# A weight transfer cut in two, and the products that fill the wait for it: gated attention and MLP decode step on one core

## The chip, the cores and the metric

One of the eight cores of a Trainium2 chip runs the kernel. The metric is the device time of one execution in microseconds (us). The kernel before takes 131.65 us (median of 3 runs, 131.53 to 131.69).

## The reference

One token (x of 576 numbers) goes through two branches, mixed by a gate: attention with 32 query heads on 16 cached key and value heads, of which the last 4096 positions are read, and an MLP with 4608 hidden units.

```python
q = x @ wq                                       # 576 -> 32 heads of 128
scores = q k^T * 128**-0.5                       # 4096 keys, two query heads per cache head
a = (softmax(scores) v).reshape(4096) @ wo       # wo: 4096 x 576
h = gelu(x @ w1 + b1)                            # 4608
b = h @ w2 + b2                                  # w2: 4608 x 576
g = sigmoid(sum(x * gate_w))
out = g * a + (1 - g) * b
```

Weights and caches are used once, in bf16. 53.6 MB come from memory; there is little arithmetic per byte.

## The kernel before: what the argument touches

All large loads go through one queue in this order: w1, wq, four tiles of K, two of V, half of w2, the third of V, the last rows of wo, the fourth of V, then the main part of wo (31 rows of 576 for each partition), then the other half of w2 in three pieces. The output y gathers in PSUM from many products. One product takes a column of 128 activations, one for each partition, and for each partition a row of 576 weights, and adds up over the partitions; it is done as two matmuls of 272 and 304 columns.

```python
    def y_add(vec, row, start=False, stop=False):
        for s in range(2):
            last = nc.tensor.matmul(
                y_out[s], lhsT=vec,
                rhs=row[:, DH:D] if s else row[:, 0:DH], ...   # cut
            )
        return last
    # ... cut: the attention, and the loads listed above
    RO = RW                                              # 31
    wo_t = big.tile([P, RO, D], BF16, name="wo_t", tag="D")
    nc.sync.dma_start(                                   # one transfer, 4464 KB
        out=wo_t[:].rearrange("p r n -> p (r n)"),
        in_=wo_src[:, 0 : 4 * RW, :].rearrange("h (a r) n -> h a (r n)", a=4),
    )
    for j0, j1 in ((0, 10), (10, 16), (16, 18)):         # w2, second half
        nc.sync.dma_start(out=w2_t[:, NJ + j0 : NJ + j1, :], in_=w2_src[:, 1, j0:j1, :])
    # ... cut: six w2 products, and the small ones that make ov from the attention's output
    late = [(gt, f, w2_t[:, f, :]) for f in range(6, NJ)]        # 12 products, loaded long ago
    wo_at = [(ov, r, wo_t[:, r, :]) for r in range(RO)]          # 31 products
    w2_at = [(gt, f, w2_t[:, f, :]) for f in range(NJ, NF)]      # 18 products
    late += [(ov_tail, j, wo_tail[:, j, :]) for j in range(4)]
    late.append(None)                                    # the unused product
    late += wo_at + w2_at
    # TensorE does `late` in this order; None is a 128 x 512 fp32 matmul
    # into a PSUM tile (spare_ps) that nobody reads
```

A product needs its row to be in SBUF, so TensorE waits, in this order, for wo and for the three w2 pieces. The list's order is forced.

## Time and profile before

| | before |
|---|---|
| span of the profiled run | 130.3 us |
| moved by DMA | 53.75 MB, 413 GB/s on average |
| TensorE busy with matmuls | 81.5 us (63%) |
| VectorE busy | 52.0 us (40%) |
| mean granted TensorE clock (share of full speed) | 0.856 |

No engine is busy throughout, but the 16 DMA engines nearly are. The lines that carry this are in the prediction and not shown again. One caution for reading them: the trace's clock records begin at 45.08 us, and up to there the views show full clock whatever it was.

### The profile page before, as it was taken

Reading aid. Unit: us, or ns where it says so; the run is one execution under the profiler, and the core shown is the slowest. Engines: PE = TensorE matmul, PEld = TensorE weight load, DVE = VectorE, ACT = ScalarE, POOL = GpSimd, SP = SyncE. Lnnn points to the kernel's source line nnn. Section 1 sums busy time; section 2 is a strip of 40 time slices with the busy share of each in tenths; the row PEclk is TensorE's granted clock in tenths of the full one; section 3 lists DMA queues with packets and bytes.
Section 4 is the critical chain, followed back from the end, with each engine's and each line's share of the span. In section 5 each row is a group of like instructions: output and inputs, shape, how many; then the busy total and the mean of one; then the engine's idle time right before and its main releaser. Section 6 shows DMA issues by size and latency. Waiting matters only on the chain.

```text
span 130.3 us, 2402 instructions
## 1 busy us (share of the span) xinstructions
PE 81.5 (63%) x1150; PEld 47.8 (37%) x1080; DVE 52.0 (40%) x48; ACT 8.3 (6%) x18; POOL 9.1 (7%) x24
## 2 busy tenths in 40 slices
PE   0019999375003998949909985985300830899994
PEld 0019949375000121211202121685300830865672
DVE  0234000400069969999999995604000020010001
ACT  2100000003000000030003003021000000000001
POOL 7049600000000000000000000000000000000000
PEclk9999999999999999999995899975555555555999
DMA  7999999899899999899999999899999989898980
GB/s 232 410 433 446 475 424 475 353 473 448 362 468 463 392 433 473 382 433 473 402 412 483 402 412 473 363 451 479 397 412 468 433 377 492 362 509 356 393 361 16
DMA packets 2364, 53.75 MB, mean 413 GB/s; under 512 B 270, under 2 KB 274, under 8 KB 564
## 3 DMA queue, kind: packets, MB, share of 16 engines
q1 hardware_dynamic: 2346, 53.61, 96.4%
q8 instruction: 8, 0.13, 0.4%
q10 hardware_dynamic: 10, 0.01, 0.0%
HBM read 53.62 MB, written 0.00 MB: 412 GB/s over the span
## 4 chain that ended last, share of the span: by engine, by line
DMA 52%; DVE 24%; PE 13%; issue 6%; SPq 2%; ACT 0%
DMA k_t<-in_A_k_cache_dram 27%; DMA w_t<-in_B_w_dram 25%; DVE kt L529 19%; PE s_ps L551 7%; PE o_ps L638 5%; DVE m L567 3%; DVE pt L600 2%; SPq L686 1%; PE y_ps L394 1%; DVE mr L570 1%; SPq L681 0%; PE mt_ps L576 0%; SPq L234 0%; ACT out_row L742 0%; SPq L230 0%
## 5 line engine op out<-in xcount | busy, mean ns | idle before, releaser
L551 PE MATMUL s_ps<-kt,qz_flat 128*128 128x512 bf16 x128 | 32.4, 410 | 17.4 <-DVE kt L529 10.6
L529 DVE STREAM_TRANSPOSE kt<-k_t 128x4096 f32<-128x4096 f32 x8 | 35.3, 4431 | 11.9 <-DMA k_t<-in_A_k_cache_dram 10.7
L638 PE MATMUL o_ps<-pt,v_t 128*128 128x8 bf16 x512 | 14.2, 167 | 16.9 <-DMA v_t<-in_A_v_cache_dram 14.9
L551 PEld LDWEIGHTS <-qz_flat 128*128 128x128 bf16 x64 | 6.8, 106 | 40.4 <-issue 38.9
L638 PEld LDWEIGHTS <-v_t 128*128 128x128 bf16 x512 | 14.1, 102 | 17.7 <-DMA v_t<-in_A_v_cache_dram 15.1
L422 PEld LDWEIGHTS <-w_t 128*128 128x128 bf16 x162 | 10.2, 165 | 0.5 <-issue 0.4
L422 PE MATMUL h_ps<-x,w_t 128*128 128x2 bf16 x162 | 10.4, 202 | 0.0
L394 PE MATMUL y_ps<-w_t,gt 128*1 128x272 bf16 (+1 forms) x72 | 8.0, 363 | 0.1
L588 ACT ACTIVATE p_t<-s_ps,negm 128x1024 bf16<-128x1024 f32 x4 | 4.5, 1114 | 50.9 <-DVE negm L584 50.9
L668 DVE RECIPROCAL rg<-mt_ps 128x32 f32<-128x32 f32 x1 | 0.4, 358 | 15.7 <-PE mt_ps L663 15.7
L343 PE MATMUL xs_ps<-ident,rows 1*128 1x1 bf16 x9 | 0.6, 189 | 9.4 <-POOL ident masks.py:199 9.4
L600 DVE STREAM_TRANSPOSE pt<-p_t 128x1024 bf16<-128x1024 bf16 x4 | 4.9, 1223 | 2.7 <-ACT p_t L588 2.7
L460 PE MATMUL q_ps<-x,wq_t 128*128 128x2 bf16 x144 | 4.0, 166 | 3.0 <-DMA wq_t<-in_A_wq_dram 3.0
L394 PEld LDWEIGHTS <-gt 128*1 128x1 bf16 x72 | 4.5, 97 | 2.2 <-issue 0.7
L567 DVE TENSOR_REDUCE m<-s_ps 128x1 f32<-128x1024 f32 x4 | 4.8, 1194 | 1.1 <-PE s_ps L551 1.1
L460 PEld LDWEIGHTS <-wq_t 128*128 128x128 bf16 x144 | 3.9, 104 | 3.0 <-DMA wq_t<-in_A_wq_dram 3.0
L743 DVE CAST out_row<-y_ps 1x272 bf16<-1x272 f32 x1 | 0.4, 429 | 11.4 <-PE y_ps L394 11.4
L431 DVE COPY hacc<-h_ps 128x36 f32<-128x36 f32 x1 | 0.2, 195 | 11.4 <-PE h_ps L422 11.4
L394 PE MATMUL y_ps<-wo_t,ov 128*1 128x272 bf16 (+1 forms) x62 | 4.2, 286 | 0.1
L343 PEld LDWEIGHTS <-rows 1*128 1x128 bf16 x9 | 0.7, 150 | 9.3 <-DVE rows L337 6.6
L394 PEld LDWEIGHTS <-ov 128*1 128x1 bf16 x62 | 3.4, 84 | 1.3 <-issue 0.8
L689 DVE TENSOR_TENSOR om<-o_ps,rgh 128x128 bf16<-128x128 f32 x1 | 0.3, 292 | 8.8 <-PE o_ps L638 8.8
(72 smaller groups left out, 38.1 us busy)
## 6 DMA issues: line engine op xcount, KB each, us to landing
k_t<-in_A_k_cache_dram SPq DMA_DIRECT2D x4, 4096.0 KB, 32.2
v_t<-in_A_v_cache_dram SPq DMA_DIRECT2D x4, 4096.0 KB, 24.9
wq_t<-in_A_wq_dram SPq DMA_DIRECT2D x1, 4608.0 KB
wo_t<-in_A_wo_dram SPq DMA_DIRECT2D x1, 4464.0 KB
w_t<-in_B_w_dram SPq DMA_DIRECT2D x1, 2880.0 KB, 14.3
w_t<-in_B_w_dram SPq DMA_DIRECT2D x1, 2592.0 KB, 23.3
w_t<-in_B_w_dram SPq DMA_DIRECT2D x1, 2304.0 KB, 8.1
w_t<-in_B_w_dram SPq DMA_DIRECT2D x1, 1440.0 KB
```

Source lines behind the costliest of these rows:

```text
L343: nc.tensor.matmul(xs_ps[:, i, :], lhsT=xdup[:, i : 2 * D : NI], rhs=ident[0:1, 0:1], start=(i == 0), stop=(i == NI - 1), skip_group_check ...
L394: last = nc.tensor.matmul(y_out[s], lhsT=vec, rhs=row[:, DH:D] if s else row[:, 0:DH], start=start, stop=stop, skip_group_check=True,)
L422: nc.tensor.matmul(h_ps[:, j:NF:NJ], lhsT=w1_t[:, i, j:FH:NJ], rhs=x2[:, i, :], start=False, stop=(i == NI - 1 and j == NJ - 1), skip_grou ...
L460: nc.tensor.matmul(q_ps[:, j : Hq : Hq // 2], lhsT=wq_t[:, i, j * Dh : (j + 1) * Dh], rhs=x2[:, i, :], start=(i == 0 and j == 0), stop=(i ...
L529: lambda: nc.vector.transpose(out=kt[g, f][:].bitcast(FP32), in_=keys.rearrange("p c d -> p (c d)").bitcast(FP32),),
L551: last = nc.tensor.matmul(s_ps[g][:, u * 512 : (u + 1) * 512].rearrange("p (c k) -> p c k", k=32), lhsT=qz(g, j, 2 * f + half), rhs=kv[:, ...
L567: queue("dve", lambda: nc.vector.reduce_max(out=m1[:], in_=s_ps[g][:], axis=AX.X))
L570: lambda: nc.vector.tensor_scalar(out=mr[:], in0=hi16[:], scalar1=m1[:, 0:1], scalar2=None, op0=ALU.mult),
L588: nc.scalar.activation(out=p_t[:].rearrange("p c k -> p (c k)"), in_=s_ps[g][:], func=ACT.Exp, bias=negm[:, 0:1], scale=SCALE, accum_out=s ...
L600: lambda: nc.vector.transpose(out=pt[:, g, :, :].rearrange("p c q -> p (c q)"), in_=p_t[:].rearrange("p c k -> p (c k)"),),
L638: last = nc.tensor.matmul(o_ps[:, 8 * g : 8 * g + 8, 0], lhsT=v_t[g][:, c, :], rhs=pt[:, g, c % 32, 8 * (c // 32) : 8 * (c // 32) + 8], st ...
L686: nc.sync.dma_start(out=w2_t[:, NJ + j0 : NJ + j1, :], in_=w2_src[:, 1, j0:j1, :])
```

## The change

Its intent: the unused product kept TensorE at work while wo was in flight. If wo comes in two transfers, its first rows are there sooner, and eight real products can do that duty. Eight more (rows 8 to 15) are held back for the later gaps, while w2 is in flight.

```diff
-    nc.sync.dma_start(
-        out=wo_t[:].rearrange("p r n -> p (r n)"),
-        in_=wo_src[:, 0 : 4 * RW, :].rearrange("h (a r) n -> h a (r n)", a=4),
-    )
+    for r0, r1 in ((0, 16), (16, RO)):
+        nc.sync.dma_start(
+            out=wo_t[:, r0:r1, :].rearrange("p r n -> p (r n)"),
+            in_=wo_src[:, 0 : 4 * RW, :].rearrange("h (a r) n -> h a (r n)", a=4)[
+                :, :, r0 * D : r1 * D
+            ],
+        )
...
-    spare_ps = ps_s.tile([P, 1024], FP32, name="spare_ps", tag="s")
-    late.append(None)
-    late += wo_at + w2_at
+    late += wo_at[0:8] + wo_at[16:RO] + wo_at[8:13] + w2_at[0:10] + wo_at[13:16] + w2_at[10:]
...   (the matmul into spare_ps goes from the loop)
```

## The prediction

> **What bounds the kernel now.** I read the 40 slices first, then the chain of waits, then the timeline of the last 20 us, then the semaphore and packet records. The slices (PE is busy share of TensorE in tenths, DMA the mean busy share of the 16 DMA engines):
>
> ```profile
> PE   0019999375003998949909985985300830899994
> PEclk9999999999999999999995899975555555555999
> DMA  7999999899899999899999999899999989898980
> ```
>
> DMA stands at 8 or 9 tenths from the second slice to the last but one; TensorE has long holes. 53.75 MB in 130.3 us is 413 GB/s. So this is a stream from memory, and a change on TensorE counts only if it shortens what follows the last byte. The chain of waits (start us, us, what) says what follows it:
>
> ```profile
> 93.11 1.53 SPq L686
> 94.64 0.05 issue
> 94.69 32.72 DMA w_t<-in_B_w_dram
> 127.41 0.04 issue
> 127.45 1.21 PE y_ps L394 x16
> 128.66 0.02 issue
> 128.69 0.40 ACT out_row L742
> ```
>
> The end is made of the landing of a piece of w2 at 127.41, then 16 matmuls (1.21 us), a copy out of PSUM (0.40 us) and the store. The products with wo are not in the chain's last part at all. The timeline of the end shows how TensorE gets there (start, busy us, instructions, idle before in brackets):
>
> ```profile
> 116.85 3.20 PE L394 MATMUL y_ps<-w_t,gt 128*1 128x272 bf16 x24
> ...
> 119.98 0.75 PE L394 MATMUL y_ps<-zeros,ov_tail 48*1 48x272 bf16 x8
> 120.66 0.30 PEld L730 LDWEIGHTS spare_ps<-p_t,ones 128*128 128x128 f32 x2 [0.27 <-issue]
> 120.66 1.13 PE L730 MATMUL spare_ps<-p_t,ones 128*128 128x512 f32 x2
> 121.72 3.76 PEld L394 LDWEIGHTS <-ov 128*1 128x1 bf16 x60 [0.76 <-issue]
> 121.90 3.78 PE L394 MATMUL y_ps<-wo_t,ov 128*1 128x272 bf16 x59
> ...
> 127.45 0.86 PEld L394 LDWEIGHTS <-gt 128*1 128x1 bf16 x15 [0.43 <-issue]
> ```
>
> The unused product (two fp32 passes) fills 120.66 to 121.79, while wo is still in flight. The first wo product starts at 121.90; the trace's semaphore records (not a line of the page) put wo's landing at 121.86. They put the three last w2 pieces at 125.32 (rows 0 to 10), 127.41 (10 to 16) and 128.08 (16 to 18). What matters is the bracket of the last line: before the last 16 matmuls TensorE already waits 0.43 us for a transfer. It has slack now.
>
> **What the Trainium skill says.** "DMA: Bandwidth & Descriptors", section "Why a DMA increments its semaphore by 16 and not by 1": each of the 16 engines ends its share with its own write to the semaphore, so a transfer is there when its slowest engine is through. The trace agrees: 270 packets under 512 B, almost all 4-byte writes, 16 to a large transfer. The same page, "Rules for kernel authors", asks for 1 MiB or more per DMA. Both new pieces, 2304 and 2160 KB, stay above that. The same page[...] fits a fixed cost of about 2.0 us per DMA; in this queue the trace does not show it between transfers: the packet records have the next transfer's first packet on an engine starting within 3 ns of the 4-byte write before it. "TensorE: Matmul & The Clock Gate", Part 1, says the clock is halved by default and is decided in free-running windows of 3413 ns. The trace agrees: one half-clock stretch is 3.413 us, another 34.133 us, ten windows. In such windows (us, then PE busy; the granted clock is the fraction ahead of the DMA share):
>
> ```profile
> 65.55:68.97 3.42, 0.66 (x4) 0.11 (x2) 3.42 (x3) 0.56 (x1) 0.00 (x0) 1.00 0.98 422
> 68.97:72.38 3.41, 3.41 (x10) 0.59 (x5) 3.41 (x1) 0.64 (x2) 0.00 (x0) 0.50 0.91 394
> ...
> 75.79:79.21 3.42, 2.06 (x11) 0.68 (x6) 3.42 (x1) 0.00 (x0) 0.00 (x0) 1.00 1.05 450
> 79.21:82.62 3.41, 3.06 (x15) 0.67 (x7) 1.60 (x3) 1.21 (x2) 0.00 (x0) 1.00 1.07 461
> ...
> 116.75:120.17 3.42, 3.42 (x31) 1.82 (x29) 0.19 (x1) 0.15 (x1) 0.00 (x0) 0.50 1.05 451
> 120.17:123.58 3.41, 3.29 (x38) 2.10 (x36) 0.00 (x0) 0.00 (x0) 0.00 (x0) 1.00 0.88 365
> ```
>
> A window with 0.66 us of matmul is followed by half clock; one with 2.06 us is not; the busy window 116.75 to 120.17 brings full clock at 120.17, before the unused product starts at 120.66.
>
> **The change, part by part.** The columns stay split 272 and 304, so no product changes shape.
>
> (1) The wo transfer of 4464 KB (128 packets of 35712 B) becomes two, 128 packets of 18432 B and 128 of 17280 B, in the same place of the queue. The bytes are the same. In the packet records of this trace a packet of 36864 B took 1364 ns and one of 18432 B 686 ns, so halving a packet costs 2 x 686 - 1364 = 8 ns. Each engine has 8 such packets and one more 4-byte write (9 ns): 8 x 8 + 9 = 73 ns, an estimate and rather high, as neighbouring records overlap by 3 to 4 ns. I take 0.06 us. All of it is on the path: everything behind wo in the queue lands that much later.
>
> (2) The first piece lands early. The V transfer ahead of it landed at 111.3; 8 packets of 686 ns are 5.5 us, so about 116.9. TensorE wants it at 120.7: no wait.
>
> (3) The unused product goes (1.13 us) and 8 products, 16 matmuls, take its place. In the wo block matmuls start every (125.49 - 121.90) / 62 = 58 ns, so 16 take 0.93 us and run from 120.7 to 121.65. TensorE then waits some 0.3 us for the second piece, at 121.86 + 0.06 = 121.92.
>
> (4) After it stand 15 + 5 = 20 products, 40 matmuls, 2.3 us, to 124.25, where before 62 matmuls ran to 125.5. TensorE then waits for rows 0 to 10 of w2 until 125.32 + 0.06 = 125.38: a new idle gap of 1.1 us.
>
> (5) 20 matmuls with w2 (1.2 us) to 126.55, then the 3 held products (6 matmuls, 0.35 us) to 126.9, then a wait of 0.5 to 0.6 us for rows 10 to 16, at 127.41 + 0.06 = 127.47.
>
> (6) The last 16 matmuls, the copy and the store are as before. The last 4 matmuls need the last piece at 128.08 + 0.06 = 128.14; TensorE reaches them after 12 matmuls, 127.5 + 12 x 0.058 = 128.2, so that piece is not the limit, though only by 0.06 us.
>
> (7) One more transfer on the SP queue shifts the round of semaphores by one. The built program shows that the last w2 piece now waits, before it is issued, for the third V transfer, which landed at 101.3. Its data are wanted at 128: nothing lost, as the queue is full till then.
>
> Sum: +0.06 us on the DMA path, about 1 us of TensorE time freed, all of it into waits. 131.65 + 0.06 = 131.7.
>
> **Rivals.** *TensorE gains count.* About 1.2 us less work stands behind wo's second piece; were TensorE the bound, the time would be near 130.5. For it: the wo block runs without a hole from 121.9 on. Against it: the 0.43 us wait at 127.45, which ends on a landing. I give it almost nothing.
>
> *The clock falls back.* TensorE now idles in three gaps (0.3, 1.1 and 0.55 us). If the window 123.58 to 126.99 were judged idle, the last 16 matmuls would run at half clock: 24 of them took 3.20 us so at 116.85, 133 ns each, or 16 x 133 = 2.1 us in place of 1.21, so 132.6. Against it: I expect 0.67 + 1.55 = 2.2 us busy in that window, above the 2.06 us that kept full clock; the windows run free of the kernel, but no gap here comes near the 2.75 us idle of the window that lost it. The eight held products are there for this.
>
> *The second transfer pays a fixed cost.* If the skill's 2 us stood open at the seam, 133.7. Against it: the packets of 3 ns distance named above. Smaller harm, 0.2 to 0.5 us, could come from an uneven pace of the 16 engines, as a half-size packet changes their phase.
>
> **Range and chances.** Three runs of before lie within 0.16 us, and my sum moves by 0.06. Below there is little room: the bytes bind. Above, the clock rival and a few tenths at the seam. I predict 131.7 us, 131.3 to 132.3 in eight cases of ten. Two per cent is 2.6 us, more than any rival makes: faster 0.01, within 0.97, slower 0.02.
>
> **What would show it.** Right: the last chain again ends with a DMA of w_t landing near 127.5 and 16 matmuls of about 1.2 us; first wo product at 120.7 with no wait; holes near 121.8, 124.3 and 127.0; granted clock 1.0 from about 120.2 to the end. Wrong: a last block of about 2 us (clock), a landing of w_t later than 127.8 (seam), or a last block that begins with no wait before it (TensorE the bound).

## The result, and the profile after

| | before | after |
|---|---|---|
| median of 6 runs each, us | 131.67 (131.53 to 131.69) | 131.73 (131.55 to 131.80) |
| ratio after / before | | 1.0004 (95%: 0.9991 to 1.0017): the same |
| DMA packets | 2364 | 2508 |
| span of the profiled run, us | 130.3 | 130.4 |

Ratios here are the mean time of one kernel's fast runs over that of the other's in the same rounds, so not quite the ratio of the medians quoted.

The chain of waits of the kernel after ends as that of before did; compare the three numbers of the landing, the block and the copy.

```profile
94.54 32.94 DMA w_t<-in_B_w_dram
127.48 0.04 issue
127.52 1.21 PE y_ps L394 x16
128.73 0.02 issue
128.75 0.40 ACT out_row L733
```

The landing is at 127.48 instead of 127.41, the block after it takes 1.21 us in both. The timeline of TensorE in the kernel after (start, busy us, instructions, idle before in brackets) shows where the rest went:

```profile
119.98 0.85 PE L394 MATMUL y_ps<-zeros,ov_tail 48*1 48x272 bf16 x8
...
120.77 3.96 PE L394 MATMUL y_ps<-wo_t,ov 128*1 128x272 bf16 x56
121.98 2.28 PEld L394 LDWEIGHTS <-ov 128*1 128x1 bf16 x38 [0.32 <-issue]
...
125.44 1.33 PE L394 MATMUL y_ps<-w_t,gt 128*1 128x272 bf16 x19 [0.71 <-DMA w_t<-in_B_w_dram]
125.44 1.12 PEld L394 LDWEIGHTS <-gt 128*1 128x1 bf16 x19 [1.05 <-issue]
...
127.52 0.86 PEld L394 LDWEIGHTS <-gt 128*1 128x1 bf16 x15 [0.58 <-issue]
```

The first wo product starts at 120.77 instead of 121.90 and follows the work ahead of it without a wait. Then come three holes, before 121.98, 125.44 and 127.52: the products done early bought waits of 0.3, 1.05 and 0.58 us. Read the weight loads (PEld) for the holes: a matmul's end is modelled, so a hole between matmuls looks shorter than the one between weight loads. In windows of 3.41 us laid on the trace's own clock events, the granted clock is full from 120.37 to the end:

```profile
116.96:120.37 3.41, 3.41 (x28) 2.12 (x26) 0.19 (x1) 0.16 (x1) 0.00 (x0) 0.50 0.98 421
120.37:123.78 3.41, 3.40 (x53) 2.60 (x50) 0.00 (x0) 0.00 (x0) 0.00 (x0) 1.00 1.01 419
123.78:127.19 3.41, 2.70 (x40) 1.87 (x36) 0.00 (x0) 0.00 (x0) 0.00 (x0) 1.00 0.85 347
```

### The profile page after: what moved, and what is told of

It reads as the page before. It is cut to its first block, busy times and chain, and to the rows that moved or that the text cites. A ratio compares the mean times of both kernels' runs of the same rounds, so it can differ in the third digit from the quotient of the medians.

```text
span 130.4 us, 2399 instructions
## 1 busy us (share of the span) xinstructions
PE 80.9 (62%) x1148; PEld 47.9 (37%) x1078; DVE 52.0 (40%) x48; ACT 8.3 (6%) x18; POOL 9.1 (7%) x24
## 2 busy tenths in 40 slices
DMA packets 2508, 53.75 MB, mean 412 GB/s; under 512 B 286, under 2 KB 290, under 8 KB 580
## 4 chain that ended last, share of the span: by engine, by line
DMA 52%; DVE 24%; PE 13%; issue 7%; SPq 2%; ACT 0%
DMA k_t<-in_A_k_cache_dram 27%; DMA w_t<-in_B_w_dram 25%; DVE kt L529 19%; PE s_ps L551 7%; PE o_ps L638 5%; DVE m L567 3%; DVE pt L600 2%; PE y_ps L394 1%; SPq L682 1%; DVE mr L570 1%; SPq L689 0%; PE mt_ps L576 0%; SPq L234 0%; ACT out_row L733 0%; SPq L230 0%
## 5 line engine op out<-in xcount | busy, mean ns | idle before, releaser
L394 PE MATMUL y_ps<-w_t,gt 128*1 128x272 bf16 (+1 forms) x72 | 7.5, 362 | 0.9 <-DMA w_t<-in_B_w_dram 0.9
```

The source lines that it names most:

```text
L394: last = nc.tensor.matmul(y_out[s], lhsT=vec, rhs=row[:, DH:D] if s else row[:, 0:DH], start=start, stop=stop, skip_group_check=True,)
```

## The experiments

The theory: the memory stream sets the end; the change puts about 0.06 us on the stream and moves TensorE's work about within its slack. The rivals: TensorE's work counts wherever it stands; the clock depends on the filled gaps; a cut costs much, and the new order hides that.

### Each half of the change alone

**split_only**: the two transfers, with the unused product and the old order.

```diff
 (the kernel before)
-    nc.sync.dma_start(out=wo_t[:]..., in_=...)
+    for r0, r1 in ((0, 16), (16, RO)): nc.sync.dma_start(...)      # as in the change
```

> The kernel before with only the wo transfer cut in two (16 and 15 rows); the unused product and the old order of products stay. Theory (the memory stream sets the end, a seam costs about 0.06 us of it): 131.67 + 0.06 = 131.7 us, the last w2 rows 10 to 16 land near 127.5, a wait of about 0.4 us stays ahead of the last 16 matmuls. Rival (a cut costs some tenths by upsetting the pace of the 16 engines, and the new order gives that back): 132.0 to 132.3 us.

Measured: 131.58 us (131.51 to 131.98, 6 runs) against 131.54 of before on the same chip; ratio 1.0003 (0.9990 to 1.0017). In its profile the landing ahead of the last 16 matmuls was at 127.25 and the block took 1.21 us: no hidden loss of the 0.3 to 0.6 us that the rival needs, and so nothing for the new order to give back. That this landing came before the 127.41 of the kernel before says that single profiles differ by more than the 0.06 us in question. One cut can't be read from one trace; wo_in_ten below measures it.

**order_only**, and the same kernel again as **order_only_b**: the new order without the unused product, wo in one transfer.

```diff
 (the kernel after)
-    for r0, r1 in ((0, 16), (16, RO)): nc.sync.dma_start(...)
+    nc.sync.dma_start(out=wo_t[:]..., in_=...)                     # one transfer, as before
```

> The changed kernel with wo in one transfer again: no unused product, the new order. TensorE idles from about 120.8 until wo lands at 121.9, then runs all it has. Theory: all of it is slack, 131.67 us within 0.1, granted clock 1.0 to the end. Rival (the unused product was needed to keep the clock up over that 1.1 us gap): half clock for a window from about 123.6 on, the wo block at some 133 ns a matmul instead of 58, about 4 us more work, and as it then runs past the landing, 133 us or more. Rival (TensorE's work counts): 130.5 to 131.2 us.

Measured: 131.70 us median, but in two groups: 131.42, 131.45, 131.68 and 131.72, and then 132.85 and 132.98. Neither answer fits: the theory gives the first group, and nothing said gave the second. Hence the repeat:

> The same kernel as order_only once more, for more executions and another profile: two of its six executions took 132.85 and 132.98 us, the other four 131.42 to 131.72, and no profile fell on a slow one. New theory (where the clock's 3.413 us windows fall against the empty stretch before wo decides it): again two groups, 131.4 to 131.8 and 132.7 to 133.1, at least one execution of the second; a profile of the second would show half clock for one window after 121.9. Rival (a disturbance of the chip in two executions): all six within 131.4 to 131.8.

Measured: 131.53, 131.56, 131.69, 131.71 and again 132.73 and 132.85. Of 12 executions 4 are slow by some 1.2 us, all of them within 0.25 us of each other; of 29 executions of the kernel before none took over 132.06. (All 12 lie within 1.5% of the fastest: 1.0032 and 1.0026 with intervals that hold 1.) This time the profile fell on a slow one. Its TensorE timeline, then its windows:

```profile
118.89 0.68 PE L394 MATMUL y_ps<-zeros,ov_tail 48*1 48x272 bf16 x8
121.81 4.89 PE L394 MATMUL y_ps<-wo_t,ov 128*1 128x272 bf16 x54 [2.23 <-DMA wo_t<-in_A_wo_dram]
```

```profile
114.39:117.81 3.42, 3.42 (x44) 2.04 (x40) 0.60 (x3) 0.15 (x1) 0.00 (x0) 0.50 0.95 402
117.81:121.22 3.41, 1.76 (x26) 1.09 (x22) 0.00 (x0) 0.00 (x0) 0.00 (x0) 1.00 0.93 401
121.22:124.63 3.41, 2.83 (x25) 2.17 (x26) 0.00 (x0) 0.00 (x0) 0.00 (x0) 0.50 0.99 408
124.63:128.04 3.41, 3.41 (x59) 2.73 (x55) 0.00 (x0) 0.00 (x0) 0.00 (x0) 1.00 0.64 257
```

The fractions 0.50 and 1.00 are the granted clock. Here the clock rose early, at 117.81, so TensorE was through with its work at 119.6 and sat idle for 2.23 us. That window, with 1.76 us of matmul, is followed by one at half clock, in which wo landed. The chain of waits of this run no longer ends on a landing:

```profile
92.40 29.36 DMA wo_t<-in_A_wo_dram
121.76 0.04 issue
121.81 7.88 PE y_ps L394 x84
```

From wo's landing on, TensorE works 7.88 us without a stop and is now the bound. In the profile of order_only, a fast execution, the clock rose 1.2 us later against the work, at 119.04, the idle stretch was 1.52 us, and the clock stayed at full. So the one slow profile shows what made that execution slow: half clock while the first wo products ran. That the idle stretch brought it is read from the order of the two windows, and that the other three executions have the same cause is inferred from their equal times. The unused product was not idle decoration: it filled most of this stretch. In the changed kernel, which differs from order_only in the cut alone, the first wo products fill it: of its executions and those of split_only and no_hold, which have the same cut, 0 of 18 are of the slow kind. The old order without the unused product was not run; the orders differ only behind wo's landing, while the stretch lies ahead of it.

### The stretch made deeper, and filled again

**gap_deep**: in order_only, six products on w2 rows that have long been loaded move from before wo's landing to after it.

```diff
 (order_only)
-    late = [(gt, f, w2_t[:, f, :]) for f in range(6, NJ)]
+    late = [(gt, f, w2_t[:, f, :]) for f in range(6, 12)]
+    held = [(gt, f, w2_t[:, f, :]) for f in range(12, NJ)]
...
-    late += wo_at[0:8] + wo_at[16:RO] + wo_at[8:13] + w2_at[0:10] + ...
+    late += wo_at[0:8] + wo_at[16:RO] + wo_at[8:13] + held + w2_at[0:10] + ...
```

> order_only with six more w2 products (12 matmuls) moved from before wo's landing to after the first 28 wo products: TensorE's empty stretch before 121.9 grows from 1.5 to about 2.5 us, the sum of its work does not change. New theory (a window with too little matmul work in it keeps or takes half clock): most or all executions at 133 to 134 us, and the profile shows granted clock 0.5 in a window after 121.9. Rival (the clock plays no part; only work behind the landing counts): 74 + 20 matmuls x 58 ns from 121.9 is 127.35, before the landing at 127.41, so 131.6 us.

Measured: 134.77 us (134.66 to 135.26, 4 runs), ratio 1.0248 (1.0224 to 1.0271), all executions slow, and by more than I had expected. Its windows:

```profile
116.61:120.02 3.41, 3.11 (x26) 1.46 (x23) 0.19 (x1) 0.15 (x1) 0.00 (x0) 0.50 1.04 449
120.02:123.43 3.41, 1.45 (x13) 1.21 (x14) 0.00 (x0) 0.00 (x0) 0.00 (x0) 0.50 0.87 362
123.43:126.85 3.42, 3.42 (x32) 2.55 (x29) 0.00 (x0) 0.00 (x0) 0.00 (x0) 0.50 0.90 371
126.85:130.26 3.41, 3.41 (x58) 2.46 (x54) 0.00 (x0) 0.00 (x0) 0.00 (x0) 1.00 0.08 30
```

The clock did not fall; it never rose, until a full window of work had passed after the landing. TensorE ran at half clock from 121.98 to 126.85, and its block after wo's landing lasted 9.65 us. The work and the stream are the same, and 3 us are lost.

**gap_filled**: gap_deep with two unused products in the stretch.

```diff
 (gap_deep)
-    late += wo_at[0:8] + ...
+    late += [None, None] + wo_at[0:8] + ...      # each None: the 128 x 512 fp32 matmul
```

> gap_deep (134.77 us) with two unused 128 x 512 fp32 products put into its empty stretch, nothing else changed: more work on TensorE, the same transfers, the same order. Theory (the stretch cost time only through the clock): full clock from about 120 on, and 131.6 to 132.0 us, some 3 us less than gap_deep although TensorE does 2.3 us more. Rival (what cost time in gap_deep was the six products moved behind wo's landing): 134.7 us or more.

Measured: 131.93, 132.45, 133.50 and 134.64 us; the last, the profiled one, counts as slow (over 1.5% above the fastest), the ratio of the other three is 1.0078 (1.0038 to 1.0119). So the filling helped, by 1.3 to 2.8 us in three executions of four against gap_deep's median, while it added work; that speaks against the rival. But my number held only for one of four. In the profiled execution the clock rose at 123.73 only, after a window with 3.41 us of fp32 matmul, and the filler itself, at half clock, held TensorE from 119.62 to 123.4, past wo's landing. A filler bought for the clock can cost what it was meant to save; products that must be done anyway add no work. I take this run as support for the clock's part, not as a clean proof.

### Are the held products needed?

**no_hold**: the changed kernel with its wo products in plain order.

```diff
-    late += wo_at[0:8] + wo_at[16:RO] + wo_at[8:13] + w2_at[0:10] + wo_at[13:16] + w2_at[10:]
+    late += wo_at + w2_at
```

> The changed kernel with the plain order (wo rows 0 to 31, then w2 rows): the eight products are not held, all 62 wo matmuls are done by about 124.4 and TensorE is empty until w2 lands at 125.4, and again from 126.6 to 127.5. Window from 123.8 to 127.2: about 0.6 + 1.2 = 1.8 us of work. Theory (holding buys no time where the clock stays; 1.68 and 2.06 us of work a window kept full clock in the kernel before): 131.7 us. Rival (the held products are needed for the clock): some executions with the last 16 matmuls at half clock, 2.1 us instead of 1.2, 132.6 us.

Measured: 131.74 us (131.57 to 131.99, 6 runs), ratio 1.0007 (0.9993 to 1.0022), no execution near 132.6. In the profile TensorE idles longer before both w2 landings and keeps full clock from 119.02 to the end. In these six executions holding eight products back bought nothing; it is the cut that makes the difference against order_only, as it gives TensorE 16 rows to work on during wo's second half. That some alignment of the windows, seen in none of the six, would need the held products is not excluded.

### What is on the path

**behind_last**: eight wo products moved behind the last w2 product.

```diff
-    late += wo_at[0:8] + wo_at[16:RO] + wo_at[8:13] + w2_at[0:10] + wo_at[13:16] + w2_at[10:]
+    late += wo_at[0:8] + wo_at[16:RO] + w2_at + wo_at[8:16]
```

> The changed kernel with the eight held wo products moved behind the last w2 product: the same transfers and the same work, 16 matmuls more behind the last landing. Theory (only what stands behind the last landing is on the path, at 58 ns a matmul): +0.93 us, 132.6 to 132.7 us. Rival (TensorE's total work sets the end wherever it stands): 131.7 us.

Measured: 132.75 us (132.71 to 132.88, 4 runs), ratio 1.0084 (1.0068 to 1.0101), or some 1.1 us more than before, about 1.0 more than the changed kernel. The chain shows it: the landing stays, the block grows from 1.21 to 2.25 us.

```profile
94.59 32.82 DMA w_t<-in_B_w_dram
127.42 0.04 issue
127.46 2.25 PE y_ps L394 x30
```

(30 instead of 32: some matmul records are missing from a trace.) The same eight products cost nothing ahead of the landing and a full microsecond behind it.

**less_wo**: 8 rows of wo less are loaded, with the same number of products (a wrong result, on purpose).

```diff
-    for r0, r1 in ((0, 16), (16, RO)):
+    for r0, r1 in ((0, 16), (16, RO - 8)):
...
-    wo_at = [(ov, r, wo_t[:, r, :]) for r in range(RO)]
+    wo_at = [(ov, r, wo_t[:, min(r, RO - 9), :]) for r in range(RO)]
```

> Wrong result on purpose: the second wo transfer brings 7 rows instead of 15, and the products of the missing rows use the last row there is, so TensorE's work is the same and 8 x 576 x 2 x 128 = 1.18 MB less is moved. Theory (the stream sets the end): [...]1.18 MB take 2.7 us, so about 129.0 us; if TensorE then comes on the path (its products between 121 and 127 need 62 + 36 matmuls x 58 ns = 5.7 us from 120.8, so 126.5 plus the gaps) a little more, up to 129.6. Rival (TensorE's chain of products sets the end): within 0.3 us of 131.7.

Measured: 129.50 us (129.10 to 130.31, 4 runs), ratio 0.9831 (0.9811 to 0.9850). With 1.18 MB less the time falls by 2.2 us on average, not by the whole 2.7 (an estimate from 36864 B in 1364 ns on each of 16 engines). The four executions differ by 1.2 us, and the profile is of the slowest of them, 130.31. Its chain tells what held that one up: the landing is gone from its end.

```profile
111.12 0.05 issue
111.16 3.57 PE o_ps L638 x128
...
116.72 10.55 PE y_ps L394 x115
127.27 0.02 issue
127.30 0.40 ACT out_row L733
```

TensorE now works without a stop from the landing of the last V tile to the end, and its last matmul ends at 127.27 instead of 128.73. So in this execution TensorE becomes the bound once 1.46 us are gained: that was its slack. The clock rose at 120.58 in it, much as at 120.38 in the changed kernel's profile. The other three executions are another 0.67 to 1.21 us shorter, so the slack is no fixed figure. In other profiles the clock rises as early as 117.70, which would let TensorE be through earlier, but none of the three was profiled, and this reason is not shown.

### What a cut costs, and what it can be worth

**wo_in_ten**: wo in ten transfers, nine of 3 rows and one of 4.

```diff
-    for r0, r1 in ((0, 16), (16, RO)):
+    for r0, r1 in ((0, 3), (3, 6), (6, 9), (9, 12), (12, 15), (15, 18), (18, 21), (21, 24), (24, 27), (27, RO)):
```

> The changed kernel with wo in ten transfers instead of two: the dose of the seam raised by eight. Theory: eight more seams at 0.05 to 0.07 us each, all on the stream: +0.4 to +0.6 us over the changed kernel, 132.1 to 132.3 us. Rival (the cut costs nothing, and the 0.07 us later landing in the changed kernel's trace is scatter): 131.7 us. Rival (each transfer has a fixed cost[...] that is in part exposed): over 134 us.

Measured: 132.11 us (131.99 to 132.22, 5 runs), ratio 1.0039 (1.0027 to 1.0051), which is 0.51 us over before for nine cuts, or 0.057 us each (0.039 to 0.075 by the interval; that all nine cost the same is assumed). The landing ahead of the last block moved to 127.96, which is 0.55 us later than the 127.41 of before, or 0.061 us a cut:

```profile
115.56 12.40 DMA w_t<-in_B_w_dram
127.96 0.04 issue
128.00 1.21 PE y_ps L394 x16
```

**one_last_piece**: the last two pieces of w2 in one transfer.

```diff
-    for j0, j1 in ((0, 10), (10, 16), (16, 18)):
+    for j0, j1 in ((0, 10), (10, 18)):
```

> The changed kernel with the last two pieces of w2 (rows 10 to 16 and 16 to 18) in one transfer: one seam fewer on the stream (-0.06 us), but the last 16 matmuls can start only when all 8 rows are there, at 128.15 - 0.06 = 128.09 instead of 127.48. Theory (a cut is worth the TensorE time that it takes from behind the last landing): +0.6 us, 132.3 us. Rival (cuts are worth nothing here, as that of wo was): 131.7 us.

Measured: 132.26 us (132.10 to 132.54, 4 runs), ratio 1.0051 (1.0032 to 1.0069), some 0.6 us more than the changed kernel's ratio of 1.0004. The landing was at 128.06 and the block after it took the same 1.21 us. This cut, if it costs the stream as much as one in wo (it was not measured by itself), earns ten times its price, because it lets 12 of the last 16 matmuls run before the last bytes are there.

None of these runs points to a version that beats both kernels: the changed one is as fast as before, and every departure tried that keeps all the bytes is equal or slower.

## Why the prediction was right

The time was right (131.7 predicted, 131.73 measured), and so was the mechanism. By its steps:

- **(1) The cut.** 0.06 us predicted; 0.057 to 0.061 us each in wo_in_ten, where the dose is large enough to trust. The 0.07 us in the changed kernel's trace agrees by luck, as profiles of one stream differ by more. In detail it was not the packet times alone: 18432 B and 17280 B took 691 and 644 ns after, together 14 ns over the 1321 of the whole one, where I had reckoned 8. That makes 8 x 14 + 9 = 121 ns; the overlap of neighbouring packets, 3 to 4 ns at each of nine more joints, takes some 30 of it back, and the rest of the difference stays unexplained.
- **(2), (3) The first piece.** Its landing was predicted for 116.9 (the sum as written, 111.3 + 5.5, gives 116.8) and recorded at 116.86; the first product for 120.7, found at 120.77; the wait for the second piece was put at 0.3 us, and is 0.32.
- **(4), (5) The new gaps.** 1.1 and 0.5 to 0.6 us predicted, 1.05 and 0.58 found. The landings of the last three pieces were predicted for 125.38, 127.47 and 128.14 and recorded at 125.40, 127.48 and 128.15. Agreement to some hundredths is in part luck: with the same transfers split_only's profile has them at 125.15, 127.25 and 127.95.
- **(6), (7)** The last block is 1.21 us as before. The later issue of the last piece had no effect to be seen.
- **TensorE gains count**: refuted by behind_last against the changed kernel (the same work, a microsecond apart by its place) and by less_wo, where the time follows the bytes until TensorE's slack is used up (1.46 us in the profiled execution). The prediction's own sum for this rival was off: only eight products, 16 matmuls or 0.93 us, no longer stand behind wo's second piece, not 1.2 us, since the three held ones still do.
- **The seam pays a fixed cost**: refuted by wo_in_ten. The skill's 2.0 us, which its section "Anatomy of one DMA" gives, is fitted for transfers issued on another path than these (see the last section).

One thing the prediction did not see, though it did not enter the number. It noted that the clock had risen before the unused product started, and looked for danger from the clock only in the gaps that the change makes; no_hold, whose gaps are longer, took no harm in six executions. The danger was in the gap that the change *closes*: with neither the unused product nor the cut, a third of the executions took 1.2 us more, and the one that was profiled had lost the clock. So "The eight held products are there for this" named, by these runs, the wrong products. It is the first eight, taken ahead of the second transfer, that fill the stretch. And the prediction's pair of windows (half clock after 0.66 us of matmul, full clock after 2.06) is no rule to lean on: 1.76 us lost the clock in order_only_b, and 1.61 us kept it in behind_last (the first line below). The prediction also left out a window of its own trace (the second line, with the window that followed): TensorE counts as busy throughout, mostly with matmuls of 8 columns, and half clock follows.

```profile
124.20:127.62 3.42, 1.61 (x24) 1.17 (x25) 0.00 (x0) 0.00 (x0) 0.00 (x0) 1.00 0.75 304
...
82.62:86.03 3.41, 3.41 (x123) 3.09 (x121) 1.46 (x2) 0.00 (x0) 0.00 (x0) 1.00 0.88 375
86.03:89.45 3.42, 1.45 (x41) 1.39 (x39) 1.24 (x2) 1.20 (x2) 0.00 (x0) 0.50 1.06 447
```

Busy time from modelled matmul ends does not decide it; what does stays open. Whether the changed kernel has a rare slow execution of its own can't be said from its 6 runs and the 12 of split_only and no_hold, the slowest of which took 131.99.

## What to carry to other kernels

In a kernel bound by a stream, ask of each product on which side of the last landing it stands: here eight products were free ahead of it, and behind it they cost a microsecond. A cut in a transfer has a price (0.06 us here) and is worth having where it takes work from behind the last landing, or where it gives TensorE real work in a hole that would cost it the clock. A median can hide such a hole: look at all executions, and if they fall into two groups, get a profile of the slow one.

## What the Trainium skill lacked or had wrong

- "TensorE: Matmul & The Clock Gate", section "HAM oscillation — how this bites in real kernels", gives "no PE-idle gaps >~3.4µs" as the abstract rule. Here a gap of 2.23 us was followed by a whole window at half clock (order_only_b), in 4 of 12 executions with equal times if the other three have the same cause. Its Part 1 says rightly that the windows run free of the kernel: the clock rose at 117.81 in one execution of that kernel and at 119.04 in another, whose work ended 0.8 us later. What share of work within a window keeps or gets the clock it does not say; by the profile's busy time it was no plain threshold (1.61 us kept it, 1.76 us lost it, and 3.41 us, mostly of 8-column matmuls, lost it in the kernel before; 3.11 us failed to raise it in gap_deep).
- "DMA: Bandwidth & Descriptors", section "Anatomy of one DMA", gives a fixed cost of about 2.0 us per DMA, fitted on another issuing path. For one more transfer in a queue that is already full no page has a figure: the runs show 0.057 us (time) to 0.061 us (landing) for each.
